# A new order list for attention with a rational feed-forward layer, constants loaded as one row, and the last stores cut into one transfer per batch

## The chip, the cores and the metric

The kernel runs on one core of one Trainium2 chip. The metric is the device time of one execution in microseconds (us); the median of three runs of the kernel before is 725.13 us (724.81 to 725.22). TensorE is PE, its weight loads PEld, VectorE DVE, ScalarE ACT, GpSimd POOL, and SyncE, which issues the DMAs here, SP.

## The reference

For each of 8 batches and 8 heads, 512 tokens (`x`, 64 wide) and 32 state vectors attend to each other both ways; the two results, 544 rows of 512 per batch, go through a feed-forward layer with a rational function between two products.

```python
scores = scale * np.matmul(x, state.transpose(0, 1, 3, 2))      # softmax over the 32 states
xread = np.matmul(a, state)
scores2 = scale * np.matmul(state, x.transpose(0, 1, 3, 2))     # softmax over the 512 tokens
sread = np.matmul(a2, x)
...
h = x @ w_in                                                    # x: the 8*544 rows of 512; d_ff = 2048
P = a[0] + a[1] * h + a[2] * h2 + a[3] * h3
Q = 1.0 + np.abs(b[0]) * np.abs(h) + np.abs(b[1]) * h2
g = P / (Q + 1e-06)
return (g @ w_out).astype(np.float32)
```

## The kernel before

Work is cut into 72 steps: 8 batches of 512 tokens by 8 slices of 256 hidden columns, then 8 steps (64 to 71) for all 256 state rows at once. Step n belongs to batch n // 8 and slice n % 8. There is no loop: a list of tokens, `ORDER`, names every operation, and the program calls them one after another (lines 954 to 965). A token is a name and its numbers, as `F:12:0`. Each engine works through its own instructions in the order of the list and waits only for what an instruction needs, so the list fixes the order on every engine and on SP's DMA queue.

Of a step n (b its batch, u its slice):

- `X:i` (i = 4u + e, line 681) multiplies the states of batches 2e and 2e+1 by slice u of w_in, giving the merged weight m of two batches; `XA` copies it out of PSUM, `xs` stores it to memory. For batch 0 it is used at once (`fh` on ACT and `fo` on DVE split it into a high and a low part); for the others `lm` loads it back and `fs` (ACT) and `ft` (POOL) split it.
- `F:n:0`, `F:n:1` (line 749): 6 matmuls each, h = m times the attention weights (`aT`).
- The rational function: `FC`, `FB`, `qa`, `ln`, `ex` on ACT; `mu`, `qd`, `po`, `g1`, `g2`, `g3` on DVE; `gl` on POOL. `g1` gives the high part gh, `gl` the low part.
- `mh:n:t` (4 matmuls from gh) and `ml:n:t` (2 from gl) add to the output tile of 128 rows t; after the eighth slice `fl` copies it out of PSUM (into `o_sb`, one of four buffers) and `os` stores it.
- Attention of batch b: `scores`, `sc_copy`, `row_T`, `row_max`, `row_sub`, `row_exp`, `row_sum`, `row_norm`, `a_T`, `a_hi`, `a_lo` for one direction, `col_*`, `e2_T`, `e2_copy`, `sread`, `sr_*` for the other. Batch 0 has its own halves with a 0 in the name.

The weights come as 64-bit words. `lr:g` loads group g (1 MB, two transfers), `cp` (ACT, two parts), `jr` and `jl` (DVE) make 32-bit floats; w_in slices stay in one of three `win_sb` buffers and are stored by `ws`, later reloaded by `lw`; w_out is split by `wh` (ACT) and `wl` (POOL) and stays. Groups 0, 1, 2, 4, 6, 8, 10, 12 are w_in, the others w_out. `lx` loads the next half batch of x or its transpose into one of two buffers; `ls` loads states; `lc` loads the six constants, each to all 128 partitions.

`X`, `F` and the attention products share two PSUM buffers in turn (tag `h`), so each waits until the readers of the one before the last are done: for `F`, that is `FC`, `FB`, `mu`, `qd`, `po`.

Of the kernel before, what the change touches and what calls it, by code (L numbers as in the profile page):

```python
# [9 lines left out]
F32 = mybir.dt.float32  # L10
# [17 lines left out]
    "e2_T0:1 fo:0 a_hi0:0 lr:3 xs:1 a_hi0:1 jl:1 e2_copy0:1 a_lo0:1 X:4 ws:1 a_lo0:0 cp:2:0 col_eps:0 "
    "F:0:0 fh:1 jr:2 cp:2:1 fo:1 lr:4 F:0:1 col_norm:0 jl:2 XA:4 F:1:0 xs:4 ws:2 FB:0 FC:0 F:1:1 qd:0 "
    "cp:3:0 cp:3:1 jr:3 qa:0 jl:3 lr:5 ln:0 mu:0 wh:3 po:0 FB:1 wl:3:1 sread:0:0 ex:0 qd:1 wl:3:0 "  # L30
    "sread:0:1 qa:1 lx g1:0 cp:4:0 ln:1 g2:0 mh:0:1 sr_copy:0 g3:0 FC:1 mh:0:3 ex:1 mu:1 gl:0 cp:4:1 "
    "sr_T:0 po:1 mh:0:0 sr_fin:0 cp:5:0 g1:1 cp:5:1 X:9 jr:5 jr:4 X:8 XA:9 jl:4 lr:6 lr:7 mh:0:2 fh:2 "
    "xs:9 XA:8 jl:5 ws:3 X:12 xs:8 fo:2 wh:5 ml:0:0 g2:1 F:2:0 lx fh:3 wl:5:0 fo:3 F:2:1 cp:6:0 g3:1 "
    "cp:6:1 ml:0:2 FB:2 ml:0:3 wl:5:1 ml:0:1 FC:2 jr:6 mh:1:3 cp:7:0 gl:1 qd:2 lr:8 mh:1:1 cp:7:1 "
    "mu:2 qa:2 mh:1:0 XA:12 mh:1:2 jr:7 ln:2 jl:7 lr:9 X:5 xs:12 ex:2 ml:1:2 jl:6 ml:1:3 wh:7 ml:1:1 "
# [970 lines left out]
```

## Time and profile before

| what | us |
| --- | --- |
| median of three runs | 725.13 |
| profiled execution | 728.45 |
| its span (first to last instruction) | 726.7 |
| PE busy | 678.5 (93%) |
| DVE busy | 619.6 (85%) |
| ACT busy | 521.9 (72%) |
| POOL busy | 326.4 (45%) |

The profile is one execution on the chip. Busy time is the time in which an engine has an instruction under way; matmul ends are modelled. The sums of the prediction are made against the profiled execution and carried to the median as a difference. Times in rows count from the start of the span.

### The profile page before, as it was taken

What the parts mean: (1) busy time and instruction counts of PE and PEld (TensorE: products, weight loads), DVE (VectorE), ACT (ScalarE), POOL (GpSimd) and SP (SyncE); (2) the same over time, 40 slices, a digit from 0 to 9 for tenths busy, and PEclk for the clock granted to TensorE, in tenths of its full rate; (3) what the DMA queues carried; (4) which work ended last, traced back from release to release, by engine and by line L of the source; (5) the groups of instructions that cost most, each with busy time, mean ns of one, the idle gap of its engine ahead of it and who ended that gap; (6) DMA issues with size and microseconds to landing.
All of it is one profiled execution on the core that took longest, in us unless ns stands there. A gap on an engine that the chain in (4) does not pass through costs nothing.

```text
span 726.7 us, 11538 instructions
## 1 busy us (share of the span) xinstructions
PE 678.5 (93%) x4584; PEld 525.2 (72%) x4584; DVE 619.6 (85%) x570; ACT 521.9 (72%) x632; POOL 326.4 (45%) x172
## 2 busy tenths in 40 slices
PE   3589797999999999999999999999999999999994
PEld 1366464777777767777877888788877887778883
DVE  3899978598898887969997997899999986999883
ACT  3878867787678756876877955977777866963861
POOL 0044444543444435444543436456464344665531
PEclk9989998899999999999999999999999999999998
DMA  7959875456132433343033102251042112000500
GB/s 219 385 183 368 264 276 176 129 160 200 35 116 87 149 127 103 117 163 99 14 103 131 54 20 74 88 183 35 17 159 87 31 43 73 15 29 9 166 2 29
DMA packets 49694, 85.69 MB, mean 118 GB/s; under 512 B 4072, under 2 KB 26728, under 8 KB 49640
## 3 DMA queue, kind: packets, MB, share of 16 engines
q1 hardware_dynamic: 49640, 84.95, 35.3%
q8 instruction: 36, 0.59, 0.3%
q14 instruction: 18, 0.15, 0.1%
HBM read 57.15 MB, written 27.79 MB: 117 GB/s over the span
## 4 chain that ended last, share of the span: by engine, by line
PE 76%; DVE 9%; ACT 5%; DMA 4%; issue 3%; POOL 1%; SPq 1%; DVEq 0%; POOLq 0%; ACTq 0%
PE h L772 25%; PE ps_x L687 3%; DMA raw<-in_w_in_dram 2%; PE o__2274 L844 2%; PE o__1444 L844 2%; PE o__4225 L844 2%; PE o__3593 L844 2%; PE o__4185 L844 2%; PE o__4842 L844 2%; PE o__4216 L844 2%; PE o__4849 L844 2%; PE o__4864 L844 2%; PE o__3670 L844 2%; PE o__4241 L844 2%; PE o__3656 L844 2%
## 5 line engine op out<-in xcount | busy, mean ns | idle before, releaser
L835 POOL TENSOR_TENSOR gl<-C,L 128x1024 fp32r<-128x1024 f32 (+1 forms) x71 | 186.2, 2625 | 199.2 <-DVE C L828 134.5
L772 PE MATMUL h<-aT,m 128*128 128x512 f32 x768 | 192.4, 401 | 3.3 <-ACT sT L386 3.0
L772 PEld LDWEIGHTS h<-aT,m 128*128 128x128 f32 x768 | 145.7, 192 | 40.8 <-ACT sT L386 3.5
L731 POOL TENSOR_TENSOR m<-m_sb,m 128x512 fp32r<-128x512 f32 x56 | 79.4, 1422 | 97.9 <-ACT m L727 71.1
L805 DVE SCALAR_TENSOR_TENSOR A<-A,b0a,h 128x1024 f32<-128x1024 f32 (+1 forms) x72 | 87.5, 1218 | 32.4 <-ACT C L784 22.3
L791 ACT ACTIVATE A<-h,cst 128x1024 f32<-128x1024 f32 (+1 forms) x72 | 76.8, 1066 | 51.8 <-PE h L772 38.1
L816 DVE SCALAR_TENSOR_TENSOR gh<-C,cst,L 128x1024 fp32r<-128x1024 f32 (+1 forms) x72 | 92.9, 1291 | 19.6 <-ACT L L889 18.8
L795 DVE TENSOR_TENSOR C<-C,h 128x1024 f32<-128x1024 f32 (+1 forms) x72 | 83.2, 1157 | 16.9 <-ACT C L784 7.1
L784 ACT ACTIVATE C<-h,cst 128x1024 f32<-128x1024 f32 (+1 forms) x72 | 83.0, 1153 | 20.0 <-PE h L772 18.2
L822 DVE SCALAR_TENSOR_TENSOR A<-A,gh 128x1024 f32<-128x1024 f32 (+1 forms) x72 | 94.2, 1308 | 1.2
L879 ACT ACTIVATE L<-A 128x1024 f32<-128x1024 f32 (+1 forms) x72 | 72.9, 1012 | 29.1 <-POOL gl L835 27.0
L811 ACT ACTIVATE A<-A 128x1024 f32<-128x1024 f32 (+1 forms) x72 | 72.6, 1011 | 28.5 <-DVE A L805 28.2
L828 DVE SCALAR_TENSOR_TENSOR C<-C,cst,A 128x1024 f32<-128x1024 f32 (+1 forms) x72 | 89.4, 1246 | 1.1
L799 DVE SCALAR_TENSOR_TENSOR C<-C,cst,h 128x1024 f32<-128x1024 f32 (+1 forms) x72 | 87.8, 1219 | 1.6
L889 ACT ACTIVATE L<-L 128x1024 f32<-128x1024 f32 (+1 forms) x72 | 72.9, 1012 | 1.7
L326 POOL TENSOR_TENSOR wo<-cv_r,wo 128x512 fp32r<-128x512 f32 x16 | 27.7, 1749 | 63.3 <-ACT wo L319 63.2
L687 PE MATMUL ps_x<-win_sb,st 64*32 64x256 f32 x1024 | 37.8, 407 | 11.2 <-DVE win_sb L310 5.7
L727 ACT CAST m<-m_sb 128x512 fp32r<-128x512 f32 x56 | 34.5, 616 | 12.3 <-PE h L772 10.6
L687 PEld LDWEIGHTS ps_x<-win_sb,st 64*32 64x32 f32 x1024 | 17.4, 111 | 28.0 <-issue 11.4
L699 ACT COPY xo<-ps_x 128x1024 f32<-128x1024 f32 (+1 forms) x32 | 28.8, 905 | 9.2 <-PE ps_x L687 8.4
L772 PE MATMUL h<-sh,m 128*128 128x256 f32 x192 | 24.5, 284 | 1.8 <-DVE m L743 1.1
L772 PEld LDWEIGHTS h<-sh,m 128*128 128x128 f32 x192 | 24.0, 192 | 2.9 <-DVE m L743 1.3
(241 smaller groups left out, 1122.2 us busy)
## 6 DMA issues: line engine op xcount, KB each, us to landing
m_dram<-xo SPq DMA_DIRECT2D x56, 256.0 KB, 3.2
m_sb<-m_dram SPq DMA_DIRECT2D x56, 256.0 KB, 2.7
out_dram<-o_sb SPq DMA_DIRECT2D x34, 256.0 KB, 3.0
xT_sb<-in_xT_dram SPq DMA_DIRECT2D x16, 512.0 KB, 4.4
raw<-in_w_in_dram SPq DMA_DIRECT2D x16, 512.0 KB, 7.6
x_sb<-in_x_dram SPq DMA_DIRECT2D x16, 512.0 KB, 4.4
raw<-in_w_out_dram SPq DMA_DIRECT2D x16, 512.0 KB, 6.4
win_sb<-w_in_dram SPq DMA_DIRECT2D x16, 512.0 KB, 5.0
```

Of the source, the lines that this page charges most:

```text
L687: nc.tensor.matmul(ps[k * NS : (k + 1) * NS, j, q, :], st[j * D : (j + 1) * D, 2 * e + q, k, :], win_t[u][j * D : (j + 1) * D, k, :], star ...
L731: nc.gpsimd.tensor_tensor(m[:, 1], MF.pop(n), m[:, 0].bitcast(F32), op=ALU.subtract)
L772: nc.tensor.matmul(h[:, ci * W : (ci + 1) * W], l, r, start=(q == 0), stop=(q == len(seq) - 1),)
L784: nc.scalar.activation(e["C"], e["h"], AF.Identity, scale=cst[:, 3:4], bias=cst[:, 2:3])
L795: nc.vector.tensor_tensor(e["C"], e["C"], e["h"], op=ALU.mult)
L799: nc.vector.scalar_tensor_tensor(e["C"], e["C"], cst[:, 1:2], e["h"], op0=ALU.add, op1=ALU.mult)
L805: nc.vector.scalar_tensor_tensor(e["A"], e["A"], b0a, e["h"], op0=ALU.add, op1=ALU.mult)
L816: nc.vector.scalar_tensor_tensor(e["gh"], e["C"], cst[:, 0:1], e["L"], op0=ALU.add, op1=ALU.mult)
L822: nc.vector.scalar_tensor_tensor(e["A"], e["A"], 1.0 + 1e-6, e["gh"].bitcast(F32), op0=ALU.add, op1=ALU.mult)
L828: nc.vector.scalar_tensor_tensor(e["C"], e["C"], cst[:, 0:1], e["A"], op0=ALU.add, op1=ALU.subtract)
L835: eng.tensor_tensor(e["gl"], e["C"], e["L"], op=ALU.mult)
L844: nc.tensor.matmul(O[t], e[l][:, j * W + t * P : j * W + (t + 1) * P], wo[:, k, 2 * u + j, :], start=(u == 0 and l == "gh" and k == 0 and ...
```

## The change

The list is made anew: 2,315 tokens for 2,316. `lw:0`, `lw:1` and `lw:2` are gone, `cb` and `cv` are new, all others stand in another order. The constants come as one row of six numbers; a product with a row of ones spreads them to 128 partitions in PSUM, and ACT copies them. The stores of the two last tiles, 128 rows that belong to four batches, are made as four transfers of 32 rows, in turn from ACT's and SP's queue. An unused helper (`keep_warm`) is removed. The list cut to what the text speaks of:

```diff
-    "ls:0:2 lx lx lc lr:0 lr:1 ls:2:8 scores0:0 scores0:1 lx sc_copy0:0 lx sc_copy0:1 row_T0:0 "
-    "col_max:0 row_T0:1 cp:0:0 col_scale:0 row_max0:0 col_exp:0:0 jr:0 cp:0:1 row_sub0:0 col_exp:0:1 "
-    "lr:2 jl:0 row_exp0:0 e2_T0:0 row_max0:1 cp:1:0 X:0 ws:0 row_sub0:1 cp:1:1 row_sum0:0 row_exp0:1 "
...
-    "a_lo:1 cp:15:0 ws:7 cp:15:1 X:28 cp:14:0 cp:14:1 jr:14 X:29 fh:7 jl:14 lm:8 XA:28 xs:28 fo:7 "
-    "wh:14 jr:15 X:6 XA:29 wl:14:0 lm:9 fs:8 F:7:0 lw:2 xs:29 XA:6 jl:15 F:7:1 xs:6 wl:14:1 wh:15 "
...
-    "mu:71 mh:69:0 po:71 ln:71 g1:70 mh:69:1 ex:71 g2:70 ml:69:1 g1:71 mh:70:0 g2:71 ml:68:0 ml:69:0 "
-    "g3:71 mh:71:0 g3:70 gv:71 mh:70:1 gl:70 mh:71:1 ml:70:0 ml:71:0 ml:70:1 fl:71:0 ml:71:1 os:71:0 "
-    "fv:71:1 os:71:1 "
+    "lx lr:0 cp:0:0 cp:0:1 ls:0:2 scores0:0 jr:0 lx jl:0 lr:1 ls:2:8 lc lr:2 scores0:1 sc_copy0:0 "
+    "sc_copy0:1 cp:1:0 X:0 XA:0 fh:0 col_max:0 jr:1 col_scale:0 col_exp:0:0 col_exp:0:1 row_T0:0 "
+    "row_max0:0 cp:1:1 row_sub0:0 cb row_T0:1 row_exp0:0 row_max0:1 cv fo:0 row_sub0:1 e2_T0:0 "
+    "row_sum0:0 row_exp0:1 X:2 b0a XA:2 cp:2:0 row_sum0:1 row_norm0:0 row_norm0:1 jl:1 X:3 xs:0 jr:2 "
...
+    "jl:5 F:1:0 g2:0 fh:2 XA:8 wh:5 F:1:1 fo:2 X:6 mh:0:0 mh:0:3 mh:0:2 mh:0:1 lr:6 xs:4 lr:7 ws:1 "
+    "xs:8 cp:6:0 FB:1 FC:1 jr:6 g3:0 gl:0 XA:6 qd:1 wl:5:1 wl:5:0 mu:1 cp:6:1 po:1 X:7 qa:1 ln:1 lx "
+    "X:5 xs:6 ex:1 cp:7:0 g1:1 jr:7 XA:7 lr:8 XA:5 cp:7:1 F:2:0 F:2:1 X:9 jl:6 ml:0:3 ml:0:0 mh:1:2 "
...
+    "wh:15 fs:9 ml:4:0 X:14 wl:15:1 mh:6:1 mh:6:0 ft:9 XA:14 qd:7 po:7 e2_T:1 a_T:1 e2_copy:1 g2:5 "
...
+    "ml:38:3 ml:38:1 sread:5:1 F:42:0 fs:43 ex:41 sr_copy:5 g1:41 g2:40 g3:40 g2:41 sr_T:5 ml:39:2 "
+    "fl:39:0 fl:39:2 sr_fin:5 lx F:42:1 mh:40:0 FB:42 ml:39:3 ml:39:1 mh:41:0 mh:40:2 FC:42 gl:40 "
+    "scores:6:0 lm:44 lx os:31:3 fl:39:3 ft:43 qd:42 mu:42 lm:45 mh:40:3 scores:6:1 ml:40:2 po:42 "
+    "fl:39:1 qa:42 F:43:0 ln:42 F:43:1 sc_copy:6 fs:44 g3:41 mh:40:1 FB:43 ex:42 ft:44 gl:41 "
...
+    "lm:60 F:58:0 ex:56 po:57 g1:56 ft:59 ml:54:0 F:58:1 g2:56 gl:55 mh:55:2 ml:55:2 lm:61 ml:55:0 "
+    "FB:58 FC:58 fs:60 os:47:0 fl:55:0 qa:57 fl:55:2 ml:54:1 ln:57 ml:54:3 F:59:0 F:59:1 ml:55:1 "
...
+    "mh:69:1 ml:68:1 mh:70:1 mh:70:0 g2:69 g3:70 FB:71 g3:69 FC:71 qd:71 gl:70 qa:71 ln:71 mu:71 "
+    "ex:71 gl:69 ml:70:1 po:71 ml:69:0 ml:70:0 g1:71 g2:71 g3:71 gv:71 mh:71:0 mh:71:1 ml:71:0 "
+    "fl:71:0 ml:69:1 os:71:0 ml:71:1 fv:71:1 os:71:1 "
...
     b0a = cp.tile([P, 1], F32, name="b0a")
+    row = cp.tile([1, 6], F32, name="row")
+    ones = cp.tile([1, P], F32, name="ones")
+    nc.gpsimd.memset(ones, 1.0)
...
 
     def const():
-        nc.sync.dma_start(cst[:, 0:4], ca.unsqueeze(0).broadcast_to([P, 4]))
-        nc.sync.dma_start(cst[:, 4:6], cb.unsqueeze(0).broadcast_to([P, 2]))
+        nc.sync.dma_start(row, cab.unsqueeze(0))
+
+    def spread():
+        CB[0] = ps_h.tile([P, 2, S], F32, name="ps_c", tag="h")[:, 0, 0:6]
+        nc.tensor.matmul(CB[0], ones, row, start=True, stop=True)
+
+    def const_copy():
+        nc.scalar.copy(cst, CB.pop(0))
...
         else:
             k = P // NS
-            nc.sync.dma_start(
-                out.rearrange("(b t) d -> b t d", t=T)[t * k : (t + 1) * k, S:, :], o
-            )
+            for i in range(k):
+                r = (t * k + i) * T + S
+                (nc.scalar, nc.sync)[i % 2].dma_start(
+                    out[r : r + NS, :], o[i * NS : (i + 1) * NS, :]
+                )
...
     ops = {
-        "warm": keep_warm,
         "lc": const,
+        "cb": spread,
+        "cv": const_copy,
...
-        "ca": np.asarray(inputs["moe_a"]),
-        "cb": np.asarray(inputs["moe_b"]),
+        "cab": np.concatenate([inputs["moe_a"], inputs["moe_b"]]),
```

## Rows read from the trace of the kernel before

**Rows 1.** Busy time by stretch: engines (instructions), granted clock, DMA share, GB/s.

```profile
0.00:40.00 40.00, 20.29 (x243) 13.06 (x244) 24.41 (x34) 24.70 (x37) 3.21 (x8) 0.95 0.85 296
40.00:140.00 100.00, 88.03 (x810) 61.01 (x809) 84.33 (x81) 76.10 (x98) 48.20 (x25) 0.90 0.72 245
140.00:640.00 500.00, 494.64 (x3122) 386.71 (x3121) 442.09 (x381) 374.37 (x435) 238.32 (x120) 1.00 0.28 90
640.00:717.40 77.40, 75.59 (x415) 64.44 (x413) 68.07 (x76) 46.69 (x64) 36.62 (x19) 1.00 0.15 48
717.40:726.70 9.30, 0.00 (x0) 0.00 (x0) 0.69 (x1) 0.00 (x0) 0.00 (x0) 0.77 0.18 56
```

**Rows 2.** Waits of DVE up to 125.5 us: us in total, times, longest.

```profile
DVE cm L391 <- ACT sT L518: 10.5, 1, 10.5
DVE A L805 <- ACT A L791: 4.4, 2, 3.5
DVE A L805 <- ACT C L784: 3.7, 3, 2.6
DVE cv_r L299 <- DMA raw<-in_w_in_dram: 2.0, 1, 2.0
```

**Rows 3.** Timeline at 125 us: start, duration, instruction, [idle before, releaser].

```profile
124.80 0.68 DVE L718 TENSOR_TENSOR m<-ps_x,m 128x512 fp32r<-128x512 f32 x1
...
125.53 1.96 PE L687 MATMUL ps_x<-win_sb,st 64*32 64x256 f32 x32 [1.53 <-DVE m L718]
```

**Rows 4.** Waits of PE from 140 to 640 us, the two longest.

```profile
PE ps_x L687 <- DMA win_sb<-w_in_dram: 1.6, 1, 1.6
PE o__5404 L844 <- DVE gh L816: 1.5, 1, 1.5
```

**Rows 5.** Timeline, the last instruction of a compute engine.

```profile
717.41 0.69 DVE L863 COPY o_sb<-o__5940 128x512 f32<-128x512 f32 x1 [3.37 <-PE o__5940 L844]
```

**Rows 6.** Waits of SP's queue from 715 us to the end.

```profile
SPq L1002 <- DMA out_dram<-o_sb: 6.9, 2, 4.4
```

**Rows 7.** The chain of waits up to 165 us: start, us, what.

```profile
4.70 9.73 DMA raw<-in_w_in_dram
...
101.42 0.87 PE ps_s L400 x8
...
135.28 0.93 PE o__402 L844 x4
...
161.10 1.39 PE h L772 x6
```

**Rows 8.** Groups of DVE instructions by line: count, busy us, mean ns.

```profile
L795 DVE TENSOR_TENSOR C<-C,h 128x1024 f32<-128x1024 f32 (+1 forms) x72 | 83.2, 1157 | 16.9 <-ACT C L784 7.1 <-ACT A L791 5.7 <-issue 2.3
L299 DVE TENSOR_SCALAR cv_r<-raw 128x1024 int32<-128x1024 uint32 x16 | 13.1, 823 | 2.0 <-DMA raw<-in_w_in_dram 2.0
```

**Rows 9.** Busy time by stretch at the start, columns as in Rows 1.

```profile
2.00:6.50 4.50, 0.00 (x0) 0.00 (x0) 0.00 (x0) 0.01 (x1) 0.00 (x0) 1.00 0.76 247
6.50:10.00 3.50, 2.22 (x32) 0.49 (x32) 0.00 (x0) 0.57 (x2) 0.00 (x0) 1.00 0.28 91
10.00:14.50 4.50, 1.94 (x8) 1.57 (x8) 1.98 (x3) 1.91 (x6) 0.00 (x0) 1.00 1.02 371
```

**Rows 10.** DMA issues by line: count, KB each, median us from issue to landing.

```profile
xT_sb<-in_xT_dram SPq DMA_DIRECT2D x16, 512.0 KB, 4.4
...
win_sb<-w_in_dram SPq DMA_DIRECT2D x16, 512.0 KB, 5.0
...
cst<-in_ca_dram SPq DMA_DIRECT2D x1, 2.0 KB, 7.1
```

**Rows 11.** Stores to the output: issue in ns (min/median/max), then landing of all.

```profile
L869 SPq DMA_DIRECT2D out_dram<-o_sb x32: 332/341/570, 147.6 to 680.5; - x32
...
DMA to landing us min/median/max: 2.0/3.0/5.6
```

**Rows 12.** The stretch after the last issue, columns as in Rows 1.

```profile
718.50:725.00 6.50, 0.00 (x0) 0.00 (x0) 0.00 (x0) 0.00 (x0) 0.00 (x0) 0.80 0.25 76
```

More of the change, by code (lines that the diff above doesn't have):

```diff
@@ L198, in attention_rational_ffn @@
 def attention_rational_ffn(
-    ctx: ExitStack, tc, x, xT, stT, w_in, w_out, ca, cb, out, w_in32, m32
+    ctx: ExitStack, tc, x, xT, stT, w_in, w_out, cab, out, w_in32, m32
 ):
@@ L234, in attention_rational_ffn @@
     b0a = cp.tile([P, 1], F32, name="b0a")
+    row = cp.tile([1, 6], F32, name="row")
+    ones = cp.tile([1, P], F32, name="ones")
+    nc.gpsimd.memset(ones, 1.0)
+    CB = {}
     st = cp.tile([P, B, NP, NS], F32, name="st")
     def const():
-        nc.sync.dma_start(cst[:, 0:4], ca.unsqueeze(0).broadcast_to([P, 4]))
-        nc.sync.dma_start(cst[:, 4:6], cb.unsqueeze(0).broadcast_to([P, 2]))
+        nc.sync.dma_start(row, cab.unsqueeze(0))
[4 more added lines that the diff above has]
+        nc.scalar.copy(cst, CB.pop(0))
     wo = cp.tile([P, 2, U * 2, DM], F32R, name="wo")
@@ L897, in sread_lo @@
         nc.gpsimd.tensor_tensor(SRS[1], srT, SRS[0].bitcast(F32), op=ALU.subtract)
-    def keep_warm(k):
-        w = ps_h.tile([P, 2, S], F32, name="warm", tag="h")
-        for _ in range(k):
-            nc.tensor.matmul(w[:, 0, 0:P], ident, ident, start=True, stop=True)
     ops = {
-        "warm": keep_warm,
         "lc": const,
+        "cb": spread,
+        "cv": const_copy,
         "lx": load_next_x,
```

313 rows, old and new, of the table ORDER are left out of this document.

## The prediction, made before the changed kernel was run

> **What bounds the kernel now.** I began with the table of stretches [rows 1]. From 140 to 640 us TensorE (PE) is busy 494.64 of 500 us at full granted clock: PE is the bound there. Up to 140 us it stands idle for 31.7 us (40 - 20.29 and 100 - 88.03), and 9.3 us pass at the end with nothing but one copy on any engine. So the change can act in three places: opening, middle, tail. The PE work itself stays (one 128x6 product is added).
>
> What sets the opening is in the waits of VectorE (DVE) [rows 2] and the place where PE last waits for it [rows 3]. Until 125.5 us DVE waits 10.5 us for its first operand, 2.0 for weights, 4.4 and 3.7 for ScalarE (ACT); the rest of the time it works. At 124.80 it makes the low half of the eighth step (fo:7), and PE starts X:6, whose PSUM buffer that frees, at 125.53. After that PE is idle only 5.4 us up to 640: the longest are 1.6 us for a reloaded w_in tile and 1.5 us for a gh tile [rows 4].
>
> The tail: the last copy out of PSUM begins at 717.41 [rows 5], and SyncE (SP) then waits 6.9 us for the two last stores [rows 6].
>
> **The list, opening.** I compare the two lists by the work that stands ahead of a place on each in-order engine. Units are from the chain [rows 7]: an accumulation of F (6 matmuls) 1.39 us, mh (4) 0.93, ml (2) half of that, eight transposes 0.87. In the old list the DVE work through fo:7 exceeds the PE work ahead of X:6 by more than at any other PE entry that waits for DVE. In the new list the worst entry is e2_T:1, whose buffer po:7 frees. Between these places the counts differ so. On DVE: one jr, jl, mu, qd and po more; two g2, two g3 and one a_lo fewer. Five go and five come; jr takes 0.82 us where a full-width operation takes about 1.2 [rows 8]: -0.4 us. On PE: two F, two mh more; four ml, one a_T fewer: 2.78 + 1.86 - 1.87 - 0.87 = 1.9 us more work done ahead of the wait. So PE is released with 0.4 + 1.9 = **2.3 us** less left to pay, if DVE waits as long as before.
>
> How long DVE waits: its first two waits, 12.5 us, come from the order of the loads. Now come state, both halves of xT, two broadcast constants, and only then raw 0, which lands at 14.43 [rows 7]. Between 6.5 and 10.0 us the queue moves 91 GB/s, against 371 right after [rows 9]: that is where the 256 rows of 8 or 16 bytes of the constants pass, 7.1 us from issue to landing [rows 10]. At 371 GB/s the 0.32 MB of that stretch would take 0.9 us, so the constants hold the queue for about 2.6 us. The new list issues one xT half and raw 0 first, 1.57 MB: 1.11 MB in the first 4.5 us as now, the other 0.46 MB at 371 GB/s in 1.2 us, so about 8 us (10 if other transfers overlap it). Then state and the second xT half (0.65 MB, 1.8 us), the scores and their copy: col_max at about 11.8, not 10.54, with jr and jl of raw 0 done before it; raw 1 is in by about 12.5. DVE's idle time falls from 12.5 to about 10 or 11. I take **1.5 us** of gain; bounds 0 and 4.5. The waits for ACT, 8.1 us, could go either way by some 3 us; I keep them.
>
> The added work: one memset on GpSimd before anything waits for that engine, an ACT copy of 6 columns like b0a, and a product that takes one of two PSUM buffers between X:0 and X:2. No row shows such a product; the nearest group, eight transposes, takes 0.87 us, so 0 to 0.9, and I take 0.1. Its wait is the risk: behind it in PE's queue stands the second half of row_T0, for which row_max0 waits on DVE. The row is issued as the seventh item, at some 6.5 us, and should land between 12 and 15; DVE reaches row_max0:1 after jr:1, at 14 to 16: 0 to 1 us, taken as 0. The slow clock of the opening (granted 0.90 on the mean [rows 1]; 1.2 of 2.4 GHz where it is low) follows PE's gaps; I leave its cost as it is.
>
> **The list, middle.** Three loads go: lw:0, lw:1 and lw:2, because all X products of the first three slices now run on the tile that was converted in place. What matters more is slack. In the old list the PE work from the freeing of a w_in buffer to the first use of its reload is 3.1 us for lw:1, 4.3 for lw:4 and 4.8 for lw:5, while such a load takes 5.0 us to land [rows 10]; the wait of 1.6 us is one of these. In the new list the shortest is 12.8 us (lw:70). From the end of F to the first mh of the same step the old list has a median of 16 to 19 us of PE work in steps 16 to 63, the new one 20: more cover for the chain over ACT and DVE in between. Against it: x loads are tighter. From freeing to use the new list has 6.2 us of PE work for scores:5:0 and 8.5 for scores:6:1, the old at least 10.6; such a load lands in 4.4 us at the median [rows 10], so this should just hold. And at fl:39:3 and fl:55:0 the copy out of PSUM stands right behind the store that empties its buffer; on SP that store stands behind a load of x or m. From sread:5:1, which lets that load go, to the end of ml:39:3 PE has 4.6 us of work, against two issues of about 0.3 us and 3.0 to land [rows 11]: covered; at 5.6, the longest landing, ACT would stand 1.7 us. Of the 5.4 us of idle time I take **2.2 us** as gained; bounds: all 5.4, or 3.1 lost (the two longest waits once more).
>
> **The tail.** The store of 256 KB is one transfer over 4 batches, and from 718.5 to 725.0 us the DMA engines are busy for a share of 0.25 at 76 GB/s [rows 12]: four of sixteen work. A store of the same size to 128 rows in a line takes 2.0 to 5.6 us to land, 3.0 at the median [rows 11]. The new code makes four transfers of 32 rows, two each on ACT's and SP's queue; ACT has no work behind them. The last piece is issued one issue later (0.33 to 0.57 us) than the first, at about 718.6, and lands at 721.6 where the last store now lands at about 725.7 (issued up to 718.8, 6.9 us of waiting in all): **4.0 us**. Bounds: landing in 2.0 or 5.6 us, 5.1 or 1.5; and 0 if the pieces spread no wider.
>
> The Trainium skill (DMA: Bandwidth & Descriptors, Why a DMA increments its semaphore by 16 and not by 1) says that a transfer runs on the largest number up to 16 that divides the outermost dimension of both sides. For 4 batches that is 4, and the trace's share of 0.25 agrees; for 32 rows it would be 16, which no row here shows. The same page (Bandwidth) speaks against the change: it wants transfers of 1 MiB, and has 0.95 us for 64 KB. Taken one after another, eight pieces would be an estimated 7.6 us, and the tail would gain nothing; the 256 KB stores of [rows 11], at 3.0 us with issue and latency, speak for less.
>
> **Sum.** -2.3 - 1.5 + 0.1 - 2.2 - 4.0 = -9.9 us. The profiled execution took 728.45 us (span 726.7), the median of the runs is 725.13; on the span this gives 716.8, on the median **715.2 us**.
>
> **The rivals.** (1) A new list brings as many waits as it removes: DVE and ACT take turns in the opening, and the 3.8 us there and the 2.2 in the middle go to other waits. For it: DVE and ACT are busy 84 and 76 of 100 us there [rows 1]. Only the tail stays: 721.1 us. (2) The pieces of the store use no more engines than the whole: the tail gains 0, the rest holds: 719.2. (3) Slower: in the opening ACT becomes the engine that DVE waits for. The new list puts X copies and conversions on ACT earlier; at F:2 ACT's work leads PE's by 10.6 us, in the old list by 8.4 at most. If DVE waits 2.6 us (the longest wait for C [rows 2]) at each of eight steps, that is 20.8 us in place of 8.1: +12.7, and the time is 727.9. It turns slower than before when these waits pass 18 us. Against it: raw tiles arrive earlier, so ACT can convert while it waits. (4) Such waits eat just the gain: 725.
>
> **How the numbers follow.** The forecast gets 0.56, rival 1 0.20, rival 2 0.07, rival 3 0.11, rival 4 0.06. The predicted time is the forecast's, 715.2. The best ends (4.5 at the start, 5.4, 5.1 and 2.2 in the list) give 708; rivals 1 and 2 lie inside; I end the range at 725, which leaves out rival 3. A measurement of this kernel can tell about 0.2%, 1.45 us: faster 0.83, within 0.06, slower 0.11.
>
> **What would show it.** Tail: with the last copy, under 6 us to the end instead of 9.3, with a DMA share well above 0.25. Start: jr:0 before 11 us, no stretch of 3 us at 91 GB/s. Opening: PE's idle time up to 140 us near 28. Middle: idle under 4 us from 140 to 640, none of it by a w_in load. I am wrong if DVE's waits for ACT up to 125 us exceed 12 us, if flushes wait for stores, or if the tail keeps 9 us.

## The result and the profile after

The changed kernel takes 702.25 us at the median (700.40 to 702.93) beside 725.17 us for the kernel before (four runs, 724.81 to 727.84): a ratio of 0.967, 95% interval 0.964 to 0.970, or 22.9 us less. The prediction had 9.9 us less, 715.2 us, and a range from 708 to 725. The sign and the places were right; the forecast gain was less than half of the measured one. The profiled execution took 702.93 us (span 701.1), that of before 728.45 (span 726.7), so the two traces stand 25.6 us apart: the profiled execution of before was 3.3 us above its median.

Busy time by stretch in the changed kernel, to be read against [rows 1] (columns as there). PE is idle for 26.1 us up to 140 us instead of 31.7, for 0.8 instead of 5.4 from 140 to 640, and runs without a break behind that; from 40 to 140 us the granted clock is 0.98 instead of 0.90.

```profile
0.00:40.00 40.00, 22.33 (x332) 13.03 (x333) 25.61 (x37) 26.82 (x46) 3.34 (x9) 0.87 0.95 315
40.00:140.00 100.00, 91.54 (x809) 66.93 (x808) 91.06 (x88) 84.13 (x103) 49.00 (x28) 0.98 0.72 243
140.00:640.00 500.00, 499.17 (x3125) 392.14 (x3124) 449.48 (x387) 374.63 (x436) 236.03 (x122) 1.00 0.27 86
640.00:692.00 52.00, 52.00 (x307) 45.99 (x306) 43.89 (x57) 31.76 (x50) 21.89 (x14) 1.00 0.23 72
692.00:701.10 9.10, 4.75 (x20) 3.20 (x18) 3.54 (x5) 0.59 (x1) 0.00 (x0) 0.97 0.22 58
```

What VectorE (DVE) waits for up to 119 us, the answer to [rows 2] (us in total, times, longest). Its first operand now comes at 8.4 us, not at 10.5. The waits for ACT's A and C, 8.1 us before, are down to 2.2; new waits stand in their place (gh, cv_r, win_sb, 7.5 us).

```profile
DVE cv_r L309 <- DMA raw<-in_w_in_dram: 9.0, 3, 8.4
DVE gh L826 <- ACT L L901: 3.0, 3, 1.4
DVE cv_r L320 <- ACT cv_y L300: 2.4, 2, 2.2
DVE win_sb L320 <- DMA w_in_dram<-win_sb: 2.1, 1, 2.1
DVE cm L401 <- ACT sT L528: 2.0, 1, 2.0
DVE A L815 <- ACT C L794: 1.3, 2, 0.7
DVE C L805 <- ACT A L801: 0.9, 1, 0.9
```

The timeline where PE last meets VectorE, the answer to [rows 3]: row_sub:1 (L444) frees a buffer at 107.78 us and F:7 starts, after 0.92 us of waiting; po:7 (L809) ends at 119.00. The first matmul of e2_T:1 (L410), the place that the prediction named, starts at 118.64, 0.36 us before that recorded end and without a wait on record: PE and VectorE come to this place together, and the row by itself doesn't show that po:7 held PE.

```profile
106.55 1.23 DVE L444 TENSOR_TENSOR e<-ps_s,mx 128x1024 f32<-128x1024 f32 x1
...
107.92 2.98 PE L782 MATMUL h<-aT,m 128*128 128x512 f32 x12 [0.92 <-DVE e L444]
...
117.72 1.28 DVE L809 SCALAR_TENSOR_TENSOR C<-C,cst,h 128x1024 f32<-128x1024 f32 x1
118.64 1.03 PE L410 MATMUL ps_e<-ident,e 128*128 128x128 f32 x8
```

From 140 us to the last matmul one wait of PE is left, against [rows 4]; none is for a load.

```profile
PE h L782 <- ACT xo L709: 0.8, 1, 0.8
```

The tail, first in the timeline (the answer to [rows 5]): the pieces are issued on two queues, and from the start of the last copy to the end pass 4.3 us, before 9.3.

```profile
696.49 1.82 SPq L884 DMA_DIRECT2D out_dram<-o_sb  x4
696.49 1.88 ACTq L884 DMA_DIRECT2D out_dram<-o_sb  x4
696.81 0.69 DVE L873 COPY o_sb<-o__5979 128x512 f32<-128x512 f32 x1 [1.76 <-PE o__5979 L854]
```

SP's last wait is 1.8 us instead of 6.9 [rows 6]:

```profile
SPq L1008 <- DMA out_dram<-o_sb: 1.8, 3, 1.5
```

And behind the last issues the DMA engines are busy for a share of 0.52 at 137 GB/s instead of 0.25 at 76 [rows 12]:

```profile
697.40:701.10 3.70, 0.00 (x0) 0.00 (x0) 0.10 (x1) 0.00 (x0) 0.00 (x0) 0.94 0.52 137
```

**PE's loss at equal work.** Idle time in a window compares different work once one kernel runs ahead. So I line up the traces by work: each unit of PE (an F half, an mh, an X ...) counts with its usual length at the full clock (1.38 us, 0.93, 1.02 ...), and the loss at a unit is its start time less the work ahead of it. The table gives the loss, in us, when so much work is done; the whole work is 651 us. Rows with the same list in the opening differ by up to 4 us from one execution to the next (at 55 us of work from 36.9 to 40.8); that is how sharp this reading is.

| kernel | 14 | 45 | 55 | 75 | 85 | 150 | 300 | end of PE |
| --- | --- | --- | --- | --- | --- | --- | --- | --- |
| before | 26.0 | 31.2 | 39.2 | 40.3 | 49.2 | 51.2 | 58.3 | 66.2 |
| tail_only (old list) | 27.0 | 32.2 | 39.0 | 40.5 | 46.8 | 48.9 | 55.8 | 63.7 |
| list_only (new list) | 24.7 | 31.4 | 33.6 | 35.8 | 36.4 | 37.4 | 41.3 | 44.2 |
| after | 23.1 | 32.8 | 34.5 | 36.7 | 37.2 | 38.3 | 42.5 | 45.2 |
| old_loads | 24.2 | 32.3 | 34.5 | 36.8 | 37.3 | 38.3 | 42.6 | 45.2 |
| cast_later | 25.6 | 31.0 | 35.7 | 38.5 | 45.8 | 47.8 | 53.1 | 61.1 |
| dve_before | 26.5 | 31.6 | 36.9 | 39.8 | 50.4 | 52.5 | 57.8 | 65.7 |
| dve_open | 21.9 | 30.8 | 32.8 | 35.0 | 41.8 | 42.8 | 45.9 | 48.7 |
| old_open_new_rest | 27.4 | 34.0 | 40.8 | 42.3 | 50.4 | 70.0 | 74.6 | 77.5 |
| new_then_old_67 | 24.8 | 29.8 | 32.1 | 44.1 | 52.8 | 56.5 | 62.0 | 69.9 |

The reader is to see two things. Up to 45 us of work (some 77 us of time) the lists are level: whatever the early loads bring is gone by then. The opening is won in two steps, around F:5 (45 to 55) and around X:28, X:6 and F:7 (75 to 85): by tail_only and list_only 4.6 and 5.7 us. Over the rows with the old list there the loss is 5.3 to 8.0 us from 45 to 55 and 6.3 to 8.9 from 75 to 85; over those with the new list it is 1.7 to 2.2 and 0.5 to 0.6 (the two dve rows left out of the second step, where work was added). And from 85 to the end the old list loses 17 us more, the new one 8.

### The profile page after: what moved, and what is told of

Read it like the earlier page. It is cut to its first block, busy times and chain, and to the rows that moved or that the text cites. A ratio compares the mean times of both kernels' runs of the same rounds, so it can differ in the third digit from the quotient of the medians.

```text
span 701.1 us, 11549 instructions
## 1 busy us (share of the span) xinstructions
PE 669.8 (96%) x4586; PEld 521.3 (74%) x4586; DVE 613.6 (88%) x570; ACT 517.9 (74%) x633; POOL 310.3 (44%) x173
## 4 chain that ended last, share of the span: by engine, by line
PE 86%; ACT 5%; DMA 4%; DVE 2%; issue 1%; SPq 1%; ACTq 0%; DVEq 0%
PE h L782 27%; DMA m_dram<-xo 3%; PE ps_x L697 3%; PE o__3021 L854 2%; PE o__2350 L854 2%; PE o__4803 L854 2%; PE o__1548 L854 2%; PE o__6006 L854 2%; PE o__4263 L854 2%; PE o__4194 L854 2%; PE o__2345 L854 2%; PE o__2991 L854 2%; PE o__4224 L854 2%; PE o__2998 L854 2%; PE o__4814 L854 2%; PE o__3700 L854 2%
## 5 line engine op out<-in xcount | busy, mean ns | idle before, releaser
L845 POOL TENSOR_TENSOR gl<-C,L 128x1024 fp32r<-128x1024 f32 (+1 forms) x71 | 176.6, 2488 | 256.2 <-DVE C L838 177.3
L782 PEld LDWEIGHTS h<-aT,m 128*128 128x128 f32 x768 | 142.9, 188 | 42.4 <-issue 3.7
L826 DVE SCALAR_TENSOR_TENSOR gh<-C,cst,L 128x1024 fp32r<-128x1024 f32 (+1 forms) x72 | 95.5, 1327 | 17.3 <-ACT L L901 17.0
L741 POOL TENSOR_TENSOR m<-m_sb,m 128x512 fp32r<-128x512 f32 x56 | 80.8, 1448 | 61.0 <-ACT m L737 31.6
L821 ACT ACTIVATE A<-A 128x1024 f32<-128x1024 f32 (+1 forms) x72 | 72.7, 1013 | 23.1 <-DVE A L815 22.9
L809 DVE SCALAR_TENSOR_TENSOR C<-C,cst,h 128x1024 f32<-128x1024 f32 (+1 forms) x72 | 87.5, 1216 | 2.3 <-ACT A L801 1.2
L336 POOL TENSOR_TENSOR wo<-cv_r,wo 128x512 fp32r<-128x512 f32 x16 | 23.5, 1488 | 41.2 <-ACT wo L329 41.2
L300 ACT ACTIVATE cv_y<-raw 128x512 f32<-128x512 f32 x32 | 21.4, 680 | 8.3 <-DMA raw<-in_w_in_dram 8.2
```

The costliest lines, as they stand in the source:

```text
L741: nc.gpsimd.tensor_tensor(m[:, 1], MF.pop(n), m[:, 0].bitcast(F32), op=ALU.subtract)
L782: nc.tensor.matmul(h[:, ci * W : (ci + 1) * W], l, r, start=(q == 0), stop=(q == len(seq) - 1),)
L809: nc.vector.scalar_tensor_tensor(e["C"], e["C"], cst[:, 1:2], e["h"], op0=ALU.add, op1=ALU.mult)
L826: nc.vector.scalar_tensor_tensor(e["gh"], e["C"], cst[:, 0:1], e["L"], op0=ALU.add, op1=ALU.mult)
L845: eng.tensor_tensor(e["gl"], e["C"], e["L"], op=ALU.mult)
```

## The experiments

Times are medians beside the kernel before on the same chip; ratios are to that kernel, with the 95% interval.

### The parts one by one

**tail_only**

```diff
-            nc.sync.dma_start(out...[t * k : (t + 1) * k, S:, :], o)
+            for i in range(k):   # one batch, 32 rows, each
+                (nc.scalar, nc.sync)[i % 2].dma_start(out[r : r + NS, :], o[...])
```

> The kernel before with the last stores alone changed. Forecast's theory: the tail is a term of its own, -4.0 us by the forecast, -4.7 us by the two traces (from the last matmul to the end 9.3 us before, 4.6 after): 720.4 to 721.1 us, a ratio of 0.993 to 0.995, and a DMA share well above 0.25 behind the last copy. Rival (the pieces spread no wider, and the shorter tail of the changed kernel comes from what else is in flight there): 725 us and a share near 0.25 again.

720.31 us, ratio 0.9934 (0.9905 to 0.9962): 4.8 us (2.8 to 6.9). SP's last wait fell to 1.8 us, as in the changed kernel, and the DMA share from 714.6 us to the end is 0.42. The tail is a term of its own, and the forecast of 4.0 holds.

```profile
SPq L1004 <- DMA out_dram<-o_sb: 1.8, 2, 1.4
```

**list_only**

```diff
-ORDER = old
+ORDER = new, without cb and cv; lc loads the broadcasts of before
```

> The new list with the constants loaded by broadcast as before (where the new list has its load) and the last stores as before. Theory A (the list is the change): 725.2 - 22.9 + 4.7 = 707.0 us, at most 1 us more for the constants. Theory B (what paid in the opening is the row of constants, which takes 256 small descriptors off the queue): the opening keeps little of its 12 us, 714 to 717 us.

707.86 us, ratio 0.976 (0.9725 to 0.9796): 17.4 us. Theory A holds; the list is three quarters of the change.

**const_only**

```diff
-... cp:1:0 X:0 ...
+... cp:1:0 cb cv X:0 ...     (lc loads the row)
```

> The kernel before with the constants alone changed: one row, the product and the copy right ahead of X:0. Theory A: raw 0 lands up to 2.6 us earlier, but VectorE, PE and ACT still take turns behind it: 0 to -2.6 us, 722.5 to 725.2. Theory B (the broadcast is what the opening lost by): -8 us or more, below 717.

722.86 us, ratio 0.9973 (0.9952 to 0.9994): 2.0 us (0.4 to 3.5), as theory A has it. The stretch of 3.5 us that ran at 91 GB/s [rows 9] now moves 329 GB/s, and jr:0 starts at 12.02 us, not 14.54. So the broadcasts did hold the queue for about 2.5 us, and by the median the old list passes most of that on. The three parts add up to 24.2 us against 23.8 for all (0.9672). Each part is known to some 2 us, and at that precision they just add.

```profile
6.50:10.00 3.50, 2.47 (x34) 0.74 (x35) 0.00 (x0) 1.02 (x3) 0.00 (x0) 1.00 1.01 329
```

**pairs**

```diff
-            for i in range(k):          # [32 rows] each
+            for i in range(0, k, 2):    # [2 batches, 32 rows] each, ACT then SP
```

> The changed kernel with two transfers of two batches each for a tile (one on ScalarE's queue, one on SP's) in place of four of one batch. If the tail gains because each piece is spread by its 32 rows over all engines, a piece whose slowest dimension is 2 goes over two engines: share 0.25 again (two queues of two), the tail back at 8 to 9 us and the time at 706 to 707 us. If it gains because there are more and smaller transfers on two queues: about half of the 4.7 us, 704 to 705.

712.42 us, ratio 0.9822 (0.9781 to 0.9863): about 11 us worse than the changed kernel, and 4.6 us worse than list_only with its whole transfers. SP waits 12.5 us for the last stores:

```profile
SPq L1010 <- DMA out_dram<-o_sb: 12.5, 2, 9.5
```

Meanwhile the share is 0.13, two of sixteen engines (columns as in [rows 1]):

```profile
703.00:706.00 3.00, 0.00 (x0) 0.00 (x0) 0.00 (x0) 0.00 (x0) 0.00 (x0) 0.50 0.13 52
```

The first theory holds in kind, but not its 706 to 707 us: it gave each queue two engines of its own, for a share of 0.25. So it is the spread over engines that pays, not the number of transfers or queues. A transfer with 4 batches outermost kept four engines busy [rows 12], with 2 batches two; with 32 rows the share is 0.52 on the mean of the stretch. The Trainium skill (DMA: Bandwidth & Descriptors, Why a DMA increments its semaphore by 16 and not by 1) has it that the largest number up to 16 which divides the slowest dimension of both sides is used, and on these queues always the lowest-numbered engines. Both agree here: four transfers on two queues shared the same two engines. The 0.95 us for 64 KB of the Trainium skill (DMA: Bandwidth & Descriptors, Bandwidth), measured there on loads that GpSimd issues, would give an estimated 7.6 us for the eight pieces one after another; here, in the changed kernel, all were down within 4.6 us of their first issue.

### The list: opening, middle and seams

**old_open_new_rest**

```diff
 old list through F:8:1, with lw:0, lw:1, lw:2
-the rest in the old order
+the rest in the new order
```

> The old list through F:8:1 (some 132 us), then what is left in the order of the new list (the three loads lw:0 to lw:2 stay, since they lie ahead); old constants, old stores. By the traces PE loses 9.0 us less behind 140 us in the changed kernel (6.7 up to 640 us, 2.4 behind). Theory A (what the middle gains comes from the order of the middle itself): 716 to 718 us. Theory C (the middle gains because it inherits the lead that the new opening gives VectorE and ACT): the gain shrinks to less than 4 us, 721 to 725.

736.23 us, ratio 1.0155 (1.0114 to 1.0196): slower, which no theory had. The table shows where: 19.6 us are lost between 85 and 150 us of work. Right behind the seam PE waits for the w_in tile of X:14, whose reload stands only just ahead of it in SP's queue, behind the stores of X:7, X:10 and X:11, which the new order has done long before:

```profile
PE ps_x L692 <- DMA win_sb<-w_in_dram: 9.3, 1, 9.3
```

From 150 on it loses 7.5 us, as the changed kernel does (6.9) and unlike the old list (14.8). That speaks for theory A behind the seam; the time itself says nothing on it.

**old_then_new_300** and **new_then_old_300**

```diff
 the one list through F:28:1 (some 320 us)
-its own rest
+the rest in the order of the other list
```

> The old list through F:28:1 (some 320 us), then what is left in the new order; old constants and stores. No w_in tile is in use across this seam, as was the case at the earlier one. Behind 280 us PE loses 9.9 us by the trace of before and 3.8 in the changed kernel. Theory A (the middle gains where its own order is new): 719.0 to 720.5 us. Theory C (the middle inherits a lead from the new opening): 724 to 725 us.

> The mirror: the new list through F:28:1, then what is left in the old order; old constants and stores. The new list alone gave 707.9 us. Theory A: the 4.5 to 6 us of the later part are lost again, the rest stays: 712.5 to 714 us. Theory C: the lead from the opening lasts: below 710 us.

722.38 us, ratio 0.9951 (0.9928 to 0.9974), and 712.46 us, ratio 0.9804 (0.9775 to 0.9832): 3.6 and 14.2 us, together 17.8, the 17.4 of list_only. Each is known to some 2 us. The mirror lies at theory A's edge, the other between A and C. So the late part gains by its own order, whatever ran before, and less than A had it; up to F:28 the list is worth 14 us.

**old_loads**

```diff
-lx lr:0 cp:0:0 cp:0:1 ls:0:2 scores0:0 jr:0 lx jl:0 lr:1 ls:2:8 lc lr:2 ...
+ls:0:2 lx lx lc lr:0 lr:1 ls:2:8 cp:0:0 cp:0:1 scores0:0 jr:0 jl:0 lr:2 ...
```

> The changed kernel with the first loads put back to the old order: state, both halves of xT, the constants (now one row), then raw 0 and raw 1. Theory A (the order of the loads is the start's own term, and VectorE starts as much later as raw 0 lands later): 1.5 to 3 us lost, 704 to 705.5 us. Theory E (the early raw tile is what the whole new opening is built on): 8 us or more lost, above 710. If the load order does nothing: 702.3.

702.61 us, ratio 0.9675 (0.9649 to 0.970): nothing lost. VectorE starts 2.8 us later (11.17 us instead of 8.38), yet at 55 us of work the loss is the same.

```profile
11.17 0.69 DVE L313 TENSOR_SCALAR cv_r<-raw 128x1024 int32<-128x1024 uint32 x1 [11.17 <-DMA raw<-in_w_in_dram]
```

So the order of the first loads is not what pays; none of the three expectations but the last holds.

**new_then_old_67**

```diff
 new list through g3:2, the token ahead of X:16 (some 67 us)
-the rest in the new order
+the rest in the old order, without lw:0, lw:1, lw:2
```

> The new list up to the third product group of its third step (some 67 us: X:0 to X:12 and jl:8 are done), then what is left in the old order without lw:0, lw:1 and lw:2; old constants and stores. With the seam at 320 us the same mixture gave a ratio of 0.980 (712 us). Theory H (the opening is won in the first 67 us, where the new list keeps the DMA engines busier and makes the reloads needless): 711 to 715 us, the old order from 67 to 320 us costs little. Theory G (it is won by the order between 67 and 130 us, where PE lost 8.7 us around X:28, X:6 and F:7): 719 to 723 us.

733.39 us, ratio 1.0094 (1.0062 to 1.0126): slower by 6.8. Between 55 and 85 us of work it loses 20.7 us; the old list loses 7.8 to 10.0 there behind its own start (tail_only, before), the new one 2.8. The largest wait is F's for the split of its X product. Theory H falls: the first 67 us don't win the opening by themselves. But G's time is missed by 10 us, so this shows as well that an order is made for the state that its own beginning leaves, and that two halves of lists can't be priced apart at such a seam.

```profile
PE h L777 <- DVE m L723: 9.7, 2, 8.4
```

**old_defer**

```diff
-lw:0 ... X:3 ... X:2 ... lw:1 jl:12 ... X:28 ... fo:7 ... X:6 F:7:0
+jl:12 ... lw:1 ... po:6 X:28 ... fo:7 ... X:6 F:7:0 lw:0 ... po:11 X:3 X:2
```

> The old list with one knot undone: X:2 and X:3 with their reload lw:0 stand behind po:11 (they are wanted from step 32 on), so that the buffer for jl:12 is free; jl:12 stands behind F:6:1, X:28 and fo:7 behind po:6; lw:1 stands behind xs:21. Nothing is left out. Theory W (reloads hold the w_in buffers, so jl:12, X:28 and with them F:7 come some 12 us later than their raw tile allows): PE's losses of 8.7 us from 117 to 132 us fall by 4 to 7 us, 718 to 721 us. Theory V (VectorE's work ahead of F:7 sets the time whatever its order): under 1.5 us either way, 723.5 to 726.5.

732.51 us, ratio 1.0083 (1.0056 to 1.0111): slower by 6.0. The move of two X products takes 2 us of PE work from ahead of F:7; X:6 now waits for a_lo (3.7 us) and F:7 for the copy of X:29 (3.3), and the loss from 75 to 85 is 10.4 us instead of 6.3 to 8.9. Theory W's gain is not there, and theory V's range doesn't hold either. What the free buffer is worth by itself this run can't say, since the move also took PE's work from ahead of the wait.

```profile
PE ps_x L692 <- DVE aT L497: 3.7, 1, 3.7
PE h L777 <- ACT xo L704: 3.3, 1, 3.3
```

**more_bytes_after** and **more_bytes_before**

```diff
-lr:4 ... lr:5 ... lr:6 ... lr:7
+lr:4 de:0 ... lr:5 de:1 ... lr:6 de:2 ... lr:7 de:3   (de: w_out to a scratch tensor, 512 KB)
```

> The changed kernel with four more transfers on SP's queue, 512 KB each from DRAM to DRAM, behind the loads of raw 4 to 7. In the changed kernel the DMA engines are busy for a share of 0.94, 0.96, 0.93 and 1.02 in the four stretches of 20 us up to 80 us, and move 313 to 355 GB/s. Theory H (the bytes set the new opening): 2.1 MB at 340 GB/s are 6.2 us, so 707 to 709 us. Theory V (an engine sets it): under 1.5 us, 702 to 704.

> The same four transfers in the kernel before, behind its loads of raw 4 to 7. There the share is 0.67 from 40 to 60 us (0.34 in its first half), so some 6 us of the queue stand empty. Theory H: most of the 6.2 us fit there, 725.5 to 728. If the old opening is set by bytes as well: 731.

705.37 us, ratio 0.9712 (0.9676 to 0.9748), and 729.93 us, ratio 1.0052 (1.0032 to 1.0071): 2.9 us more than the changed kernel, known to some 3.5, and 3.8 (2.3 to 5.1) more than the one before. The first is not clear of noise (the four runs took 702.42 to 706.43 us), and both lie between their theories. So some of the bytes come out in the old list; that the new list feels them less or more is not shown, and by the median theory H's 707 to 709 us is not reached.

### Who sets the end of the opening

**no_low_before**

```diff
-        nc.gpsimd.tensor_tensor(wo[:, 1, f, :], ..., op=ALU.subtract)
+        pass     (wo[:, 1] is set to zero once)
```

> The kernel before without GpSimd's 16 subtractions for the low half of w_out (one memset at the start stands for them), so the low half of w_out is left out of the result. Theory S (VectorE's stretched operations up to fo:7, 3.4 us more than the sum of their usual lengths, come from GpSimd's work beside them, and VectorE sets the opening): 2.5 to 4 us faster, 721 to 722.5 us, VectorE's stretch up to fo:7 under 1.5 us. Theory T (the stretch lies beside waits and costs nothing): 724.5 to 725.5 us.

726.77 us, ratio 1.0000 (0.9985 to 1.0016): nothing. In the kernel before, jr:6 takes 1.79 us while GpSimd subtracts (L326); the usual length is 0.69. Without the subtraction it takes 0.68, and VectorE then waits 1.87 us for ACT's C where it had waited 0.27. First the kernel before, then the experiment:

```profile
52.17 2.28 POOL L326 TENSOR_TENSOR wo<-cv_r,wo 128x512 fp32r<-128x512 f32 x1
53.22 1.79 DVE L299 TENSOR_SCALAR cv_r<-raw 128x1024 int32<-128x1024 uint32 x1
...
55.27 1.28 DVE L805 SCALAR_TENSOR_TENSOR A<-A,b0a,h 128x1024 f32<-128x1024 f32 x1 [0.27 <-ACT C L784]
```

```profile
53.22 0.68 DVE L300 TENSOR_SCALAR cv_r<-raw 128x1024 int32<-128x1024 uint32 x1
...
55.77 1.28 DVE L801 SCALAR_TENSOR_TENSOR A<-A,b0a,h 128x1024 f32<-128x1024 f32 x1 [1.87 <-ACT C L780]
```

The stretch up to fo:7 fell only from 3.4 to 2.3 us, since other operations were stretched instead (jr:12, 2.04 us, beside gl), and VectorE's idle time rose from 23.7 to 25.7. What is shown is that this stretch was cover for a wait; that all stretch is, is not.

That the stretch comes from GpSimd the traces show well. In the kernel before, 29 VectorE operations of the whole execution (of those that usually take 0.4 us or more) take over 0.12 us longer than their usual length. Every one of them ends a fixed time behind the end of the GpSimd operation that was under way when it began: the longer ones, 1.22 or 1.28 us by themselves, 1.08 us behind it, the shorter ones, as jr with its 0.69, 0.55 us. In jr:6 above GpSimd ends at 54.46 and jr:6 at 55.01; so do gl and jr:14 here, at 123.00 and 123.55:

```profile
119.81 3.19 POOL L835 TENSOR_TENSOR gl<-C,L 128x1024 fp32r<-128x1024 f32 x1 [5.45 <-DVE C L828]
121.82 1.73 DVE L299 TENSOR_SCALAR cv_r<-raw 128x1024 int32<-128x1024 uint32 x1
```

None of the 139 operations mu, qd and po that began beside GpSimd was stretched; these read h from PSUM. The changed kernel has 27 stretched operations in all, but in its opening, up to po:7, only one. The Trainium skill (SBUF — State Buffer, SBUF: two separate sides) says that VectorE, with two operands from SBUF (against a GpSimd operation that reads SBUF) or in its fast form, and GpSimd exclude each other for a whole instruction. The rows agree: VectorE's operation ends that long behind GpSimd's, however early it had begun.

**cast_later**

```diff
-X:20 wh:11 xs:17 ... fh:5 scores:1:1 XA:20 wl:11:0 fo:5 xs:20 sc_copy:1 g3:4 F:5:0
+X:20 xs:17 ... fh:5 scores:1:1 XA:20 fo:5 xs:20 sc_copy:1 wh:11 wl:11:0 g3:4 F:5:0
```

> The old list with one step moved: ScalarE's cast wh:11 (with wl:11:0) stands behind sc_copy:1. In the kernel before, wh:11 waits 1.3 us for VectorE's jl:11, and behind it in ScalarE's queue stand fh:5, the copy XA:20 and sc_copy:1, for which PE stands 3.0 us ahead of F:5, which then runs 4.6 us at the low clock instead of 2.75. Theory P: 2 to 4 us gained, 722 to 724 us. Theory D: PE comes to F:5 earlier and waits the longer at X:28, X:6 and F:7: within 1 us of before, the loss at 85 us of PE work stays at 46 to 49 us.

723.94 us, ratio 0.9976 (0.9954 to 0.9998): 1.7 us (0.1 to 3.3), between the theories, the interval touching both. This is the wait that went, in the timeline of tail_only, whose list is that of before: the cast waits 1.31 us, three short ACT operations stand behind it, and F:5 starts after 2.99 us and takes 4.62 us, where F:7 of the changed kernel takes 2.98 (the granted clock is 0.64 in this stretch, there 1.00).

```profile
86.27 1.04 ACT L319 CAST wo<-cv_r 128x1024 fp32r<-128x1024 f32 x1 [1.31 <-DVE cv_r L310]
87.22 0.58 ACT L714 CAST m<-ps_x 128x512 fp32r<-128x512 f32 x1
...
88.17 1.02 ACT L386 COPY sT<-ps_sc 128x1024 f32<-128x1024 f32 x1
...
89.25 4.62 PE L772 MATMUL h<-aT,m 128*128 128x512 f32 x12 [2.99 <-ACT sT L386]
```

PE's waits from 75 to 140 us, first tail_only, then cast_later: the wait for sT falls from 3.0 to 1.3 us, and the later wait for fo (m) grows from 1.4 to 2.5.

```profile
PE ps_x L687 <- DVE win_sb L310: 3.1, 1, 3.1
PE h L772 <- ACT sT L386: 3.0, 1, 3.0
...
PE ps_x L687 <- DVE m L718: 1.4, 1, 1.4
```

```profile
PE ps_x L692 <- DVE m L723: 2.5, 1, 2.5
PE ps_x L692 <- DVE win_sb L315: 2.4, 1, 2.4
...
PE h L777 <- ACT sT L391: 1.3, 1, 1.3
```

In the table the loss from 45 to 55 is 4.7 us instead of tail_only's 6.8, and that from 55 to 85 is 10.1 instead of 7.8: beside tail_only, what was won at F:5 is given back at X:28 to F:7, 14.8 and 14.6 us from 45 to 85. But tail_only has the lowest loss of the old list's rows there: before has 18.0 and old_open_new_rest 16.4, and dve_before, whose list is the same up to there, loses 5.3 from 45 to 55. So one trace can't tell theory D from P, and whether the 1.7 us come from F:5 stays open.

**dve_before** and **dve_open**

```diff
-... mu:6 ...
+... dd:4 mu:6 ...     (dd: four reductions of a constant on VectorE, nobody reads the result)
```

> The kernel before with four more VectorE operations of some 1.2 us each (a reduction of a constant, whose result nobody reads) ahead of mu:6, at some 110 us. Theory D: all of it comes out at the end, +4.9 us, 730 to 731.5 us. Theory P (PE's other waits cover it): under 2 us, below 728.

> The changed kernel with the same four operations ahead of mu:6, which there stands at 111 us. There VectorE ends po:7 at 119.0 us and PE comes to e2_T:1 at 118.4. Theory D (VectorE has just no lead left to give): +4 to +5 us, 706 to 707.5 us. If PE has become the bound by then: under 2 us, 702 to 704.

730.08 us, ratio 1.0058 (1.0031 to 1.0084), and 707.17 us, ratio 0.9746 (0.9714 to 0.9777): 4.2 and 5.4 us for 4.9 us of added work (the difference of the ratios, times 725), known to some 2 and 3 us. Theory D holds for both lists: at 110 us VectorE has no lead to give, and within these bounds what it is given comes out at the end one for one. In dve_open PE's added wait, 3.6 us, stands at X:14, one entry ahead of e2_T:1; the record names no releaser for it.

**dve_mid_before** and **dve_mid_after**

```diff
-... mu:40 ...
+... dd:4 mu:40 ...
```

> The kernel before with four more VectorE operations (the same reductions, some 4.9 us in all) ahead of mu:40, at some 470 us. Theory M1 (thin cover): 2 us or more come out at the end, 727.5 to 730.5. Theory M2 (the middle has cover in either list, its losses are single waits): under 1 us, 725 to 726.5.

> The changed kernel with the same four operations ahead of mu:40, at some 450 us. Both theories: the cover takes it, under 1 us, 702 to 703.3. If even here VectorE has no lead, +4.9 as in the opening: 707.

733.62 us, ratio 1.0104 (1.0057 to 1.0151), and 705.32 us, ratio 0.9703 (0.9666 to 0.9739): 7.5 us (4.1 to 10.9) in the old list, 2.2 in the new, known to some 3.5 us, for the same 4.9. For the old list theory M2 is out, and theory M1's 727.5 to 730.5 is passed as well. For the new list both theories had cover take the work, under 1 us; by the times that is open, and so is any difference between the lists. By the traces it is wrong. PE waits for the added work once in either, in the old list for 4.7 us (the longest of two):

```profile
PE h L779 <- DVE C L806: 5.4, 2, 4.7
```

and in the new list for 3.7:

```profile
PE ps_e L416 <- DVE r L459: 3.7, 1, 3.7
```

So the new list does not cover it at this place either. Counted as in the table, PE's loss behind 300 us of work grows by some 7 us in the old list and some 5 in the new.

## Why the prediction was right in its places and wrong in its size

**Right.** That the change acts in three places, that the list's opening matters through the last place where PE waits for VectorE (so far as dve_before and dve_open show it), and that the tail is a matter of how many DMA engines a store uses. The signs came: jr:0 at 8.4 us, no slow stretch at the start, PE idle 26.1 us up to 140, under 1 us in the middle and none of it by a load, 4.3 us of tail at a share of 0.52. Rival 2 is out by tail_only and pairs. Rival 3 (ACT takes the pace) is out: the waits for ACT up to 119 us are 10 us with all forms counted, and VectorE is busy for 39.5 of the 40 us from 80 to 120, before 34.5. Rivals 1 and 4 are out by list_only.

**The tail**: 4.0 forecast, 5.0 by the traces (9.3 less 4.3), 4.8 by tail_only. The mechanism and the size were right.

**The constants**: the 2.6 us that they hold the queue were right (jr:0 came 2.5 us earlier by them alone). The end gains 2.0 us in the old list. In the new one no gain is clear of noise: list_only and the tail's term give 703.1 us by themselves, 0.8 above the changed kernel.

**The start**, -1.5 us: the size of VectorE's first waits was right (12.5 before, 11.0 after), but old_loads shows that the new list doesn't pass them on. The term as the prediction argued it, from the order of the loads to the end of the kernel, is not there.

**The list, opening**, -2.3 us: this step failed, in one term. The prediction set PE's release equal to VectorE's time up to the last place less PE's work ahead of it. The places were fo:7 and po:7, as forecast, each VectorE's 103rd token. Before: 125.5 - 79.3 = 46.2. After: 119.0 - 81.3 = 37.7. So 8.5 us where 3.8 stood for list and start. PE's work ahead: 2.0 us more, forecast 1.9. VectorE's idle time: 23.7 (the four waits that the prediction named are 20.6 of it) to 21.7, 2.0 less, forecast 1.5 less. VectorE's busy time: 101.8 to 97.3, 4.5 less, forecast 0.4 less. I had priced operations at their mean and taken the mean as a property of the operation. It is a property of the order: by their usual lengths the two sets differ by 0.7 us, and the other 3.8 are nearly all operations stretched beside GpSimd in the old list (3.4 us), of which the new one has hardly any. The group that I read for jr's price [rows 8] held it: 823 ns of mean, where 14 of the 16 took 0.69. The same shows in g3, up to 125 us; in the kernel before (count, busy us, mean ns):

```profile
L828 DVE SCALAR_TENSOR_TENSOR C<-C,cst,A 128x1024 f32<-128x1024 f32 x7 | 9.8, 1406 | 0.1
```

and g3 and jr in the changed kernel:

```profile
L309 DVE TENSOR_SCALAR cv_r<-raw 128x1024 int32<-128x1024 uint32 x16 | 11.3, 706 | 9.2 <-DMA raw<-in_w_in_dram 9.0
...
L838 DVE SCALAR_TENSOR_TENSOR C<-C,cst,A 128x1024 f32<-128x1024 f32 x6 | 7.7, 1281 | 0.0
```

That is where the missing term stands in the equation; that the end of the opening came earlier because of it is only argued. no_low_before shows that a stretch can be worth nothing, because VectorE would have waited for ACT instead. What is shown is narrower: ahead of this place VectorE's time counts about one for one (dve_before, dve_open), and the early loads (old_loads) don't tell the lists apart. How much PE's own waits on the way count (cast_later), and the bytes (more_bytes), stays open.

**The clock.** "I leave its cost as it is" put a second term at nothing, and the old list pays for it where the new one doesn't. Times here run from the start of a group of matmuls to the start of the next; for the two halves of F, 2.76 us is usual. Behind a wait of 3.0 to 3.2 us of PE, F:5 took 4.3 to 5.3 us at a granted clock of 0.50 to 0.63 in six traces of the old list (before, tail_only, no_low_before, old_then_new_300, dve_mid_before, old_open_new_rest); in a seventh, dve_before, behind the same wait, 2.9 us at 1.00. F:7, behind X:6, for which PE had waited too, took 4.1 to 4.9 us at 0.55 to 0.68 in four of the six, and 2.9 us at 1.00 in tail_only and no_low_before. In the changed kernel and in list_only either takes 2.7 to 2.8 us. So the slow clock costs the old list 1.5 to 2.5 us at F:5 in six of seven traces, and 1.3 to 2.1 at F:7 in four of six. F:7 stands behind the last large wait, and its part should reach the end; how much of F:5's does is open, since PE waits for VectorE behind it. First the kernel before behind X:6, then tail_only at F:5, then the changed kernel at F:7 (columns as in [rows 1]):

```profile
125.50:132.50 7.00, 6.96 (x45) 4.70 (x46) 2.86 (x2) 3.84 (x5) 6.33 (x5) 0.55 0.86 263
89.20:93.90 4.70, 4.65 (x13) 3.69 (x14) 3.25 (x3) 1.14 (x2) 4.70 (x3) 0.64 0.99 354
107.90:110.90 3.00, 2.98 (x13) 2.50 (x14) 3.00 (x3) 2.88 (x3) 2.23 (x2) 1.00 0.95 373
```

**The middle**, -2.2 us, bounds 5.4 gained and 3.1 lost: too small, and the bounds were too. From 85 us of work to the end PE lost 17 us before (17.0 and 16.9 in two traces) and 8 after. Two errors. I took 2.2 of the 5.4 idle us [rows 4] as gained, and 4.5 were. And I took the idle time from 140 to 640 us for all that PE lost: behind 640 us PE stood another 1.8 us ([rows 1]: 75.59 of 77.40), now nothing, and the rest, some 2.7 us, is spread over many units and stands in no list of waits. old_then_new_300 confirms 3.6 us of it behind 320 us. Why the new order has fewer such waits is not settled. Cover, the prediction's reason, is not borne out by the dve_mid pair: in either list the added work shows as a wait. The slack of 3.1, 4.3 and 4.8 us ahead of lw:1, lw:4 and lw:5 counts the X product that frees the buffer, 1.0 us, as well; the comparison with the new list stands without it.

So of the 13 us that the forecast missed, the opening's VectorE term is by this account about 4 to 5, the middle and end about 7, the tail about 1, and F:7's clock up to 2; these don't add up exactly, since executions of one kernel differ by some us.

## What to carry to other kernels

Compare two orders by the loss at equal work, not by idle time in windows, over several executions of each, and before pricing a move ask whether the engine that sets the pace gets it: 4.9 us given to VectorE came out about whole. A wait can cost more than its length: F:5 waited 3 us and then took 1.5 to 2.5 us longer. An operation's mean length in a profile is made by its neighbours too; take its usual length and count the stretched ones apart. For a short last store, make the outermost dimension large: 32 rows, not 2 or 4 batches.

## What the runs showed of the hardware that I had not expected

Four transfers of 128 KB with two batches outermost, on two queues, used two engines between them: 12.5 us of waiting at no more than 52 GB/s, where eight transfers of 64 KB with 32 rows outermost took 1.8 us of waiting. One VectorE operation more than doubled its length beside GpSimd (0.69 to 1.79 us), and taking that GpSimd work away changed nothing in the time; each stretched operation ended 1.08 or 0.55 us behind GpSimd's. And two orders that are each sound can, joined, be slower than both: 733 and 736 us from lists that take 708 and 725.
